# Sign and low bits of the weights as two 16-bit halves of one word, joined in one VectorE pass; plan priorities redone

## The chip, the core and the metric

The kernel runs on one core of a Trainium2 chip. A core has five engines that work side by side, each through its own instructions in order: TensorE (PE in the profile; its weight loads are PEld), VectorE (DVE), ScalarE (ACT), GpSimd (POOL) and SyncE (SP), which here only issues DMAs. The time is device microseconds of one execution. Medians of three runs are compared; the profile is one further execution, recorded instruction by instruction.

## The reference

The inputs and weights are 64-bit floats. Eight batches of 576 positions with 8 heads of 64 go through attention with a sliding window of 64, and the result, 4608 tokens of 512, goes through a layer with 1024 hidden units:

```python
scores = np.where(mask, scale * (q @ kT), -1e9)     # 0 <= i - j < 64
attn = exp(scores - max); attn /= sum + 1e-9
x = (attn @ v) ...                                  # 4608 x 512
h = x @ w_in                                        # 512 x 1024
e = exp(h - max(h)); sm = e / (sum(e) + 1e-9)
solu = h * sm
ln = (solu - mean) / sqrt(var + 1e-6) * g_ln
return ln @ w_out                                   # 1024 x 512
```

q, k and v reach the chip as 32-bit floats; w_in and w_out reach it as raw 64-bit words, and the kernel converts them itself.

## The kernel before

The tokens are cut into 36 tiles of 128. For tile t, `scores` puts q times k into PSUM (pS), `softmax` takes the minimum of the masked and negated scores per head (DVE, tile sS), the exponential (ACT, L480) and the division by the sum (POOL, L498; DVE for tile 0). `transposes` turns the eight blocks of sS, by TensorE (L533) for tiles 0 to 3 and by DMA from tile 4 on, into PT. `values` multiplies PT by v (L559), and ACT copies the result out as xH. `moe_in` multiplies xH by w_in into pH (L590 in plain 32-bit form for tiles 0 to 2, L603 in three rounded passes from tile 3 on). `moe_norm` takes the maximum (DVE, L618), the exponential (ACT, L620), the product with its sum (DVE, L623) and the normalisation. pH has one buffer, so L590 of the next tile waits until L623 has read it. `moe_transpose` turns the result, and `moe_out` multiplies it by w_out into pO (L724 for tiles 0 and 1, L737 after).

The weights come in eight blocks of 128 rows by 1024, blocks 0 to 3 for w_in and 4 to 7 for w_out; block 0 is handled in two halves of 512. A 64-bit word has two 32-bit words, `lo` and `hi`. A 32-bit float is made from them so, in `weight_block`:

- ACT writes |hi| times a power of two into the tile w (L351, `Abs`);
- POOL multiplies hi by zero in place, which leaves its sign (L360);
- DVE clips w from above (L362), shifts it left by 3 and ORs the sign in (L365), and shifts lo right by 29 and ORs that in (L368).

From tile 3 on the products run with weights split into a rounded part H and a rest L: `split` has ACT write H (L392 for w_in, L397 for w_out) and DVE the rest (L393, L399), 16 of each.

The order of each engine is found at build time. `Plan` gets each operation with a cost; it gives each a due time back from TensorE's order, adds a number from the table HINTS for some tiles, and plays the engines through, each of which takes the ready operation that is due first. The order found is written out as it is. SP issues DMAs in one queue: q and k of a tile (qk, 640 KB), v (512 KB), weight blocks (raw, 1 MB each, four buffers), the outputs. A raw block's load into a buffer waits for the last reader of the block that was there; the load of qk of tile t waits for the scores of tile t-3.

Of the kernel before, what the change touches and what calls it, by code (L numbers as in the profile page):

```python
# [19 lines left out]
P = 128  # L20
# [16 lines left out]
    ("DVE", "rec", 0, 0): 5100, ("DVE", "w", 0, 0): 2850, ("PE", "pS", 2, 0): 800, ("POOL", "e", 0, 0): 37550,
    ("POOL", "mst", 0, 0): -6350, ("ACT", "H", 0, 1): 850, ("DVE", "sS", 0, 1): 1100, ("DVE", "w", 0, 1): 200,
    ("PE", "pS", 0, 1): -59100, ("DVE", "w", 0, 2): 6350, ("PE", "pS", 0, 2): -14500,
    ("ACT", "yH", 0, 3): 57400, ("DVE", "PT", 0, 3): -29050, ("DVE", "y", 0, 3): 26250,  # L40
    ("DVE", "e", 0, 4): 2600, ("DVE", "rec", 0, 4): -4750, ("DVE", "sS", 0, 4): -3400,
# [185 lines left out]
def tile_window_attention_solu_moe(  # L227
# [672 lines left out]
```

## Time and profile before

| | us |
|---|---|
| median of three runs | 512.44 (512.27 to 513.65) |
| the profiled execution | 512.81 |
| its span, first to last instruction | 510.6 |
| mean granted TensorE clock over the span | 0.997 |

The span is the stretch that the profile shows; about 2.2 us of the execution's time lie around it. A row of a timeline gives start, duration, engine, line, what it writes and reads, how often, and in brackets how long the engine was idle before and what it waited for. TensorE's matmuls overlap, and their ends are modelled, so what a matmul costs is read from one start to the next. An L590 product of 128 by 512 stands in the trace as two records.

### The profile page before, as it was taken

The numbers are of one execution on the slowest core, as the hardware profiler recorded it, in microseconds if no ns is written. First come the engines' busy times: TensorE is split into PE (matmuls) and PEld (weight loads), VectorE is DVE, ScalarE is ACT, GpSimd is POOL, SyncE is SP. The second block draws the span as 40 slices with busy tenths as digits, with TensorE's granted clock in tenths as the row PEclk, the third lists the DMA queues.
The fourth block names the chain that finished last, engine by engine and source line by source line (L and its number), as shares of the span: only waits on it lengthen the run. The fifth ranks groups of instructions, "written<-read, shape, count | busy, mean of one in ns | idle before, by whom it ended". The sixth has DMA issues, their size and how long they took to land.

```text
span 510.6 us, 11601 instructions
## 1 busy us (share of the span) xinstructions
PE 492.0 (96%) x4064; PEld 392.5 (77%) x4064; DVE 406.0 (80%) x1176; ACT 355.7 (70%) x960; POOL 311.4 (61%) x566
## 2 busy tenths in 40 slices
PE   2889999999999999999999999999999999999996
PEld 1445576888888888888888888888888888888885
DVE  4988997979797979797878897877888879977531
ACT  5588795868686868676776867685959586855331
POOL 4389467574757574747474858484748485945430
PEclk9989999999999999999999999999999999999999
DMA  8994346978888878687989696969795969554201
GB/s 320 418 419 164 114 110 113 249 160 147 185 218 147 227 187 217 166 219 170 219 146 248 146 246 148 247 146 234 127 268 134 248 132 232 124 125 103 83 22 42
DMA packets 150762, 94.09 MB, mean 184 GB/s; under 512 B 135088, under 2 KB 135344, under 8 KB 150320
## 3 DMA queue, kind: packets, MB, share of 16 engines
q1 hardware_dynamic: 150704, 93.35, 72.5%
q8 instruction: 32, 0.52, 0.5%
q14 instruction: 26, 0.21, 0.1%
HBM read 50.86 MB, written 9.44 MB: 118 GB/s over the span
## 4 chain that ended last, share of the span: by engine, by line
PE 92%; DVE 3%; ACT 1%; issue 0%; ACTq 0%
PE pO L737 36%; PE pH L603 35%; PE pO L559 7%; PE pS L460 6%; PE pH L590 4%; PE pO L724 3%; PE pS L700 1%; DVE mst L618 0%; ACT e L620 0%; DVE w L368 0%; DVE e L623 0%; DVE sS L475 0%; DVE yL L711 0%; DVE w L365 0%; PE pS L533 0%
## 5 line engine op out<-in xcount | busy, mean ns | idle before, releaser
L498 POOL TENSOR_SCALAR sS<-sS,rec 128x128 f32<-128x128 f32 x280 | 147.2, 544 | 11.6 <-DVE rec L496 8.1
L480 ACT ACTIVATE sS<-sS,nmx 128x128 f32<-128x128 f32 x288 | 111.4, 389 | 2.0 <-DVE nmx L475 1.9
L737 PE MATMUL pO<-w_outH,yH 128*128 128x512 f32 x272 | 108.2, 398 | 0.0
L737 PE MATMUL pO<-w,yH 128*128 128x512 f32 x272 | 106.1, 390 | 0.0
L603 PE MATMUL pH<-w_inH,xH 128*128 128x512 f32 x264 | 103.7, 393 | 0.0
L603 PE MATMUL pH<-w,xH 128*128 128x512 f32 x264 | 101.8, 389 | 0.0
L737 PE MATMUL pO<-w_outH,yL 128*128 128x512 f32 x272 | 83.9, 390 | 0.0
L512 ACT COPY raw<-sS 128x1024 uint16<-128x1024 uint16 x64 | 66.8, 1046 | 23.0 <-POOL sS L498 23.0
L603 PE MATMUL pH<-w_inH,xL 128*128 128x512 f32 x264 | 81.9, 389 | 0.0
L640 POOL TENSOR_SCALAR e<-e,mst 128x512 f32<-128x512 f32 x72 | 68.9, 966 | 3.9
L632 POOL TENSOR_SCALAR mst<-mst 128x1 f32<-128x1 f32 x36 | 17.9, 497 | 79.2 <-ACT sq L629 42.9
L618 DVE TENSOR_REDUCE mst<-pH 128x1 f32<-128x1024 f32 x36 | 44.0, 1221 | 26.7 <-PE pH L603 24.6
L522 DVE COPY PT<-raw 128x1024 uint16<-128x1024 uint16 x64 | 49.8, 788 | 17.8 <-DMA raw<-raw 17.4
L573 ACT CAST xH<-pO 128x512 fp32r<-128x512 f32 x33 | 19.3, 585 | 64.0 <-PE pO L559 63.9
L737 PEld LDWEIGHTS pO<-w_outH,yH 128*128 128x128 f32 x272 | 51.0, 188 | 12.7 <-issue 2.4
L737 PEld LDWEIGHTS pO<-w_outH,yL 128*128 128x128 f32 x272 | 51.1, 188 | 10.9
L737 PEld LDWEIGHTS pO<-w,yH 128*128 128x128 f32 x272 | 51.1, 188 | 10.0
L603 PEld LDWEIGHTS pH<-w_inH,xH 128*128 128x128 f32 x264 | 49.6, 188 | 11.1 <-issue 0.3
L603 PEld LDWEIGHTS pH<-w_inH,xL 128*128 128x128 f32 x264 | 49.6, 188 | 10.6 <-issue 0.2
L603 PEld LDWEIGHTS pH<-w,xH 128*128 128x128 f32 x264 | 49.6, 188 | 10.4 <-issue 0.2
L626 POOL TENSOR_SCALAR mst<-mst 128x1 f32<-128x1 f32 x36 | 16.2, 451 | 65.6 <-DVE mst L623 59.7
L629 ACT ACTIVATE sq<-e,mst 128x1024 bf16<-128x1024 f32 x36 | 41.4, 1150 | 19.5 <-POOL mst L626 19.5
(71 smaller groups left out, 850.5 us busy)
## 6 DMA issues: line engine op xcount, KB each, us to landing
qk<-qk SPq DMA_DIRECT2D x36, 640.0 KB, 6.0
v<-vS SPq DMA_DIRECT2D x36, 512.0 KB, 4.6
y<-ot SPq DMA_DIRECT2D x35, 256.0 KB, 2.5
raw<-w_out SPq DMA_DIRECT2D x4, 1024.0 KB, 11.6
raw<-w_in SPq DMA_DIRECT2D x3, 1024.0 KB, 11.1
raw<-raw SPq DMA_TRANSPOSE x126, 2.8
raw<-w_in SPq DMA_DIRECT2D x2, 512.0 KB, 6.0
y<-ot SPq DMA_DIRECT2D x2, 128.0 KB, 1.7
```

Of the source, the lines that this page charges most:

```text
L460: nc.tensor.matmul(PS(t, p // 2)[half * WIN:(half + 1) * WIN, r, p], q[rs, p, half * WIN:(half + 1) * WIN], keys, start=True, stop=True)
L480: plan.op("ACT", 390, lambda h=h: nc.scalar.activation(SS(t)[:, h], SS(t)[:, h], AF.Exp, bias=cols("nmx", h), scale=-1.0, accum_out=cols(" ...
L498: plan.op(engine, cost, lambda h=h: v.tensor_scalar(SS(t)[:, h], SS(t)[:, h], rec()[:, h:h + 1], 0.0, ALU.mult, ALU.add), [R], [("sS", t, ...
L512: plan.op("ACT", 1050, lambda x=x: nc.scalar.copy(XP(t)[:, x], SS(t)[:, 4 * x:4 * x + 4].bitcast(U16).rearrange("p h (n w) -> p w (h n)", ...
L522: plan.op("DVE", 740, lambda x=x: nc.vector.tensor_copy(PT(t)[:, 4 * x:4 * x + 4].bitcast(U16).rearrange("p h (n w) -> p h w n", w=2), XP( ...
L559: nc.tensor.matmul(PX(t, p)[r * D:(r + 1) * D, p, ks], V(t, half)[:, h * D:(h + 1) * D], PT(t)[:, h, ks], start=True, stop=True)
L590: plan.op("PE", 860, lambda c=c, x=x: nc.tensor.matmul(PH(t)[:, x * 512:(x + 1) * 512], XH(t)[:, c], W32(c)[:, x], start=(c == 0), stop=(c ...
L603: plan.op("PE", 235, lambda n=n, c=c, d=d, x=x, w=w: nc.tensor.matmul(PH(t)[:, d * 512:(d + 1) * 512], x(t)[:, c], WH(c, d) if w is WH els ...
L618: plan.op("DVE", 1225, lambda: nc.vector.tensor_reduce(nmax(), PH(t), axis=AX.X, op=ALU.max, negate=True), [("pH", t)], [key(0)])
L629: plan.op("ACT", 1150, lambda: nc.scalar.activation(T("sq", t, [P, DFF], BF16), E(t), AF.Square, bias=nmean(), scale=1.0, accum_out=ss()), ...
L640: plan.op("POOL", 770, lambda h=h, hs=hs: nc.gpsimd.tensor_scalar(E(t)[:, hs], E(t)[:, hs], nmean(), kk(), ALU.add, ALU.mult), [key(4), ke ...
L737: plan.op("PE", 235, lambda n=n, f=f, i=i, x=x, y=y, w=w: nc.tensor.matmul(PO(), y(t)[:, f], w(i, x), start=(n == 0), stop=(n == len(passe ...
```

## The change

ACT now makes the low bits: a pass of type Copy scales the low word, read as an unsigned number, by 2^-29 and subtracts nearly a half, so that conversion to a 16-bit integer leaves the top three bits, and writes them into the lower half of the low word. POOL writes the sign, as 16-bit float zero with a sign, into the upper half of the same word. So the low word holds sign and low bits in place, and DVE needs one pass to shift w and OR that word in. POOL's pass now waits for ACT's low pass instead of the `Abs` pass. Block 0 has its two low passes, then its two `Abs` passes. HINTS is a new table; nothing else is changed.

```diff
 HINTS = {
-    ("ACT", "H", 0, 0): -5500, ("ACT", "w", 0, 0): -5050, ("DVE", "mst", 0, 0): 11450,
...
+    ("ACT", "raw", "w", 0): -53950, ("PE", "pH", 0, 36): -89650, ("DVE", "sS", 0, 0): -45650,
...
-MASKED = (0, 1, 2, 3, 4, 5, 6, 7)
+JOINED = (0, 1, 2, 3, 4, 5, 6, 7)
...
+        def piece(y, w, dtype):
+            return raw().bitcast(dtype).rearrange("p a n (k w) -> p a n k w", w=2)[:, y, :, 0, w]
...
-            masked = i in MASKED
-            if not masked:
+            joined = i in JOINED
+
+            def absolute(x=x, ab=ab, R=R, W=W):
+                plan.op("ACT", ab, lambda x=x: nc.scalar.activation(
+                    tf()[:, x], hi()[:, x].bitcast(F32), AF.Abs, scale=EXP_SCALE), [R], [W])
+
+            if not joined:
+                absolute()
+            else:
                 plan.op("ACT", ab + 12, lambda x=x: nc.scalar.activation(
-                    lo()[:, x], lo()[:, x].bitcast(U32), AF.Copy, bias=-0.47, scale=255 / 256 * 2.0 ** -29), [R], [B])
+                    piece(x, 0, U16), lo()[:, x].bitcast(U32), AF.Copy, bias=-0.47, scale=255 / 256 * 2.0 ** -29),
+                    [R], [B])
+                absolute()
...
-                plan.op("POOL", 660, lambda y=y: nc.gpsimd.tensor_scalar(
-                    hi()[:, y].bitcast(F32), hi()[:, y].bitcast(F32), 0.0, 1.0, ALU.mult, ALU.mult), [R, W], [S + (y,)])
+                plan.op("POOL", 660, lambda y=y, joined=joined: nc.gpsimd.tensor_scalar(
+                    piece(y, 1, BF16) if joined else hi()[:, y].bitcast(F32),
+                    hi()[:, y].bitcast(F32), 0.0, 1.0, ALU.mult, ALU.mult),
+                    [R, B] if joined else [R, W], [S + (y,)])
...
-            if masked:
+            if joined:
                 plan.op("DVE", n + 200, lambda x=x: nc.vector.scalar_tensor_tensor(
-                    t()[:, x], t()[:, x], 3, hi()[:, x], ALU.logical_shift_left, ALU.bitwise_or),
-                    [R, *D], [W], port=True)
+                    t()[:, x], t()[:, x], 3, lo()[:, x], ALU.logical_shift_left, ALU.bitwise_or),
+                    [R, B, *D], [W], port=True)
+            else:
                 plan.op("DVE", n + 200, lambda x=x: nc.vector.scalar_tensor_tensor(
-                    t()[:, x], lo()[:, x], 29, t()[:, x], ALU.logical_shift_right, ALU.bitwise_or),
+                    t()[:, x], t()[:, x], 3, hi()[:, x], ALU.logical_shift_left, ALU.bitwise_or),
                     [R], [W], port=True)
```

What the change and the new table do to the order is seen at three places. In the changed file L371 is ACT's low pass, L365 its `Abs`, L378 POOL's sign, L382 the clip and L385 the join; L607 is the old L590, L550 the old L533, L477 the old L460, L576 the old L559. The number after a tile's name is the block or tile; pS_73 and pS_74 take the transposes of tiles 1 and 2.

VectorE at the weights of w_in, before (L362 clip, L365 sign, L368 low bits):

```order
L362 TENSOR_SCALAR w_1_177<-w_1_177 128x1024
L365 SCALAR_TENSOR_TENSOR w_1_177<-w_1_177,raw_1_113 128x1024
L498 TENSOR_SCALAR sS_0_137<-sS_0_137,rec_0_169 128x128
L368 SCALAR_TENSOR_TENSOR w_1_177<-raw_1_113,w_1_177 128x1024
L362 TENSOR_SCALAR w_2_206<-w_2_206 128x1024
L365 SCALAR_TENSOR_TENSOR w_2_206<-w_2_206,raw_2_115 128x1024
```

The same place now:

```order
L382 TENSOR_SCALAR w_1_225<-w_1_225 128x1024
L385 SCALAR_TENSOR_TENSOR w_1_225<-w_1_225,raw_1_113 128x1024
L382 TENSOR_SCALAR w_2_249<-w_2_249 128x1024
L385 SCALAR_TENSOR_TENSOR w_2_249<-w_2_249,raw_2_115 128x1024
L382 TENSOR_SCALAR w_3_259<-w_3_259 128x1024
```

Block 2 is finished ahead of the minima of tile 1; before, its last pass stood behind those minima and behind block 3.

TensorE from the end of tile 0's hidden product (pH_0) to tile 1's (pH_1), before:

```order
L590 MATMUL pH_0_217<-w_2_206,xH_0_213 128x512 x2
L590 MATMUL pH_0_217<-w_3_243,xH_0_213 128x512 x2
L533 MATMUL pS_73_356<-ident_73,sS_1_253 128x128 x4
L460 MATMUL pS_3_361<-qk_3_245 64x128 x16
L559 MATMUL pO_37_385<-PT_1_381,v_1_149 64x64 x8
L533 MATMUL pS_73_356<-ident_73,sS_1_253 128x128 x4
L559 MATMUL pO_73_424<-PT_1_381,v_1_149 64x64 x8
L533 MATMUL pS_74_436<-ident_73,sS_2_315 128x128 x4
L590 MATMUL pH_1_447<-w_0_140,xH_1_413 128x512 x2
```

The same place now:

```order
L607 MATMUL pH_0_251<-w_3_259,xH_0_238 128x512 x2
L550 MATMUL pS_73_347<-ident_73,sS_1_269 128x128 x4
L477 MATMUL pS_3_359<-qk_3_261 64x128 x8
L550 MATMUL pS_73_347<-ident_73,sS_1_269 128x128 x4
L576 MATMUL pO_37_381<-PT_1_357,v_1_148 64x64 x8
L477 MATMUL pS_3_359<-qk_3_261 64x128 x8
L576 MATMUL pO_73_406<-PT_1_357,v_1_148 64x64 x8
L550 MATMUL pS_74_418<-ident_73,sS_2_310 128x128 x4
L607 MATMUL pH_1_429<-w_0_168,xH_1_404 128x512
L550 MATMUL pS_74_418<-ident_73,sS_2_310 128x128 x4
L607 MATMUL pH_1_429<-w_0_168,xH_1_404 128x512
```

The scores of tile 3 are in two halves; the first still stands ahead of most of tile 1's work. The second half of pS_74, which stood behind pH_1, now stands inside it.

ScalarE from the exponential of tile 1's hidden layer (e_1) on, before:

```order
L620 ACTIVATE e_1_533,mst_1_498<-pH_1_447,mst_1_498 128x1024
L569 COPY xH_2_521<-pO_74_536 128x256
L538 COPY PT_3_567<-pS_75_547 128x512
L480 ACTIVATE sS_4_552,sm_4_570<-sS_4_552,nmx_4_553 128x128 x3
L392 CAST w_inH_98<-w_2_206 128x512
L480 ACTIVATE sS_4_552,sm_4_570<-sS_4_552,nmx_4_553 128x128 x5
L392 CAST w_inH_98<-w_2_206 128x512
L392 CAST w_inH_98<-w_1_177 128x512 x2
```

The same place now (L637 is the old L620, L586 the old L569, L497 the old L480, L646 the square, L414 the old L397, L409 the old L392):

```order
L637 ACTIVATE e_1_529,mst_1_497<-pH_1_429,mst_1_497 128x1024
L586 COPY xH_2_548<-pO_38_516 128x256
L586 COPY xH_2_548<-pO_74_531 128x256
L365 ACTIVATE w_6_559<-raw_6_341 128x1024
L365 ACTIVATE w_7_566<-raw_7_379 128x1024
L371 ACTIVATE raw_7_379<-raw_7_379 128x1024
L371 ACTIVATE raw_5_256<-raw_5_256 128x1024
L497 ACTIVATE sS_4_540,sm_4_583<-sS_4_540,nmx_4_541 128x128 x8
L646 ACTIVATE sq_1_601,mst_1_497<-e_1_529,mst_1_497 128x1024
L414 ACTIVATE w_outH_99<-w_5_495,g_sb_100 128x512 x2
L409 CAST w_inH_98<-w_0_168 128x512 x2
```

Four passes of the weight blocks now stand behind this exponential, where none stood, and all eight casts of w_in follow them; before, block 0's two casts were ahead of it.

## Rows read from the trace of the kernel before

**Rows 1.** The page: busy us (share of the span) and instructions of each engine.

```profile
PE 492.0 (96%) x4064; PEld 392.5 (77%) x4064; DVE 406.0 (80%) x1176; ACT 355.7 (70%) x960; POOL 311.4 (61%) x566
```

**Rows 2.** TensorE's waits: who waited for whom, us in total, times, longest.

```profile
PE pH L590 <- DVE w L368: 1.7, 1, 1.7
...
PE pS L460 <- PE pS L460: 0.4, 1, 0.4
```

**Rows 3.** Timeline of TensorE, 14 to 50 us: start, duration, instruction, idle before.

```profile
26.77 5.37 PE L590 MATMUL pH<-w,xH 128*128 128x512 f32 x8 [1.73 <-DVE w L368]
31.97 0.60 PE L533 MATMUL pS<-ident,sS 128*128 128x128 f32 x4
32.50 1.10 PE L460 MATMUL pS<-qk 64*64 64x128 f32 x32
33.53 0.69 PE L559 MATMUL pO<-PT,v 128*64 128x64 f32 x16
34.15 0.66 PE L533 MATMUL pS<-ident,sS 128*128 128x128 f32 x4
...
36.59 7.03 PE L590 MATMUL pH<-w,xH 128*128 128x512 f32 x16
43.46 0.60 PE L533 MATMUL pS<-ident,sS 128*128 128x128 f32 x4
...
47.70 2.84 PE L590 MATMUL pH<-w,xH 128*128 128x512 f32 x6 [0.35 <-DVE mst L623]
```

**Rows 4.** Busy time by stretch; then granted clock (PEclk), DMA share, GB/s.

```profile
24.00:27.00 3.00, 1.27 (x3) 0.47 (x4) 2.97 (x10) 2.06 (x7) 0.87 (x1) 1.00 1.03 416
27.00:30.00 3.00, 3.00 (x4) 1.04 (x4) 2.88 (x18) 2.92 (x15) 2.63 (x7) 0.51 1.02 422
```

**Rows 5.** Groups by line and form, whole span: busy us, mean ns, idle before.

```profile
L512 ACT COPY raw<-sS 128x1024 uint16<-128x1024 uint16 x64 | 66.8, 1046 | 23.0 <-POOL sS L498 23.0
...
L360 POOL TENSOR_SCALAR raw<-raw 128x512 f32<-128x512 f32 x16 | 11.9, 767 | 15.0 <-ACT w L351 15.0
L368 DVE SCALAR_TENSOR_TENSOR w<-raw,w 128x1024 int32<-128x1024 int32 x7 | 9.0, 1284 | 0.1
L365 DVE SCALAR_TENSOR_TENSOR w<-w,raw 128x1024 int32<-128x1024 int32 x7 | 8.6, 1226 | 0.5
L351 ACT ACTIVATE w<-raw 128x1024 f32<-128x1024 f32 x7 | 8.0, 1149 | 5.8 <-DMA raw<-w_in 5.4 <-DMA raw<-w_out 0.4
...
L368 DVE SCALAR_TENSOR_TENSOR w<-raw,w 128x512 int32<-128x512 int32 x2 | 1.7, 848 | 0.1
...
L351 ACT ACTIVATE w<-raw 128x512 f32<-128x512 f32 x2 | 1.3, 651 | 4.8 <-DMA raw<-w_in 4.8
```

**Rows 6.** Busy time by stretch of 10 us: PE, PEld, DVE, ACT, POOL; clock, DMA, GB/s.

```profile
20.00:30.00 10.00, 8.27 (x62) 3.88 (x62) 9.75 (x41) 8.80 (x35) 4.80 (x9) 0.85 1.03 418
30.00:40.00 10.00, 9.32 (x89) 5.61 (x88) 8.77 (x28) 8.44 (x26) 9.26 (x16) 0.98 1.02 417
...
60.00:70.00 10.00, 10.00 (x36) 6.45 (x35) 9.74 (x34) 10.00 (x27) 6.61 (x14) 1.00 0.52 138
```

**Rows 7.** ScalarE's timeline, 10.8 to 32.5 us.

```profile
10.60 0.38 ACT L480 ACTIVATE sS<-sS,nmx 128x128 f32<-128x128 f32 x1
...
12.87 0.56 ACT L538 COPY PT<-pS 128x512 f32<-128x512 f32 x1
...
19.50 1.17 ACT L351 ACTIVATE w<-raw 128x1024 f32<-128x1024 f32 x1 [3.88 <-DMA raw<-w_in]
...
24.05 0.35 ACT L569 COPY xH<-pO 128x256 f32<-128x256 f32 x1
24.84 1.14 ACT L351 ACTIVATE w<-raw 128x1024 f32<-128x1024 f32 x1 [0.45 <-DMA raw<-w_out]
```

**Rows 8.** The one qk load issued at 19.3 us (L419): its row, its landing.

```profile
L419 SPq DMA_DIRECT2D qk<-qk x1: 418/418/418, 19.3 to 19.3; - x1
...
DMA to landing us min/median/max: 10.9/10.9/10.9
```

More of the change, by code (lines that the diff above doesn't have):

```diff
@@ L35 @@
 HINTS = {
-    ("ACT", "H", 0, 0): -5500, ("ACT", "w", 0, 0): -5050, ("DVE", "mst", 0, 0): 11450,
[L37 to L41, printed above, removed]
@@ L51 @@
-    ("POOL", "sS", 0, "e"): 900,
+    ("ACT", "raw", "w", 0): -53950, ("PE", "pH", 0, 36): -89650, ("DVE", "sS", 0, 0): -45650,
+    ("ACT", "sS", 0, 0): -5250, ("DVE", "rec", 0, 0): -44950, ("ACT", "raw", "w", 1): -32750,
+    ("ACT", "raw", "w", 2): -68150, ("ACT", "PT", 0, 0): -64150, ("DVE", "sS", 0, 1): 46450,
+    ("ACT", "w", 0, 3): -82400, ("ACT", "w", 0, 4): 20250, ("ACT", "raw", "w", 5): 36650,
+    ("ACT", "w", 0, 5): 31000, ("ACT", "raw", "w", 7): 7800, ("DVE", "w", 0, 7): -2600,
+    ("PE", "pS", 0, 2): -15500, ("DVE", "sS", 0, 2): -88000, ("ACT", "mst", 0, 0): 5900,
@@ new lines @@
+    ("POOL", "e", 0, 0): 160100, ("POOL", "sS", 0, 3): 46750, ("PE", "pH", 0, 1): 30400,
+    ("ACT", "mst", 0, 1): 48650, ("POOL", "e", 0, 1): 65650, ("ACT", "PT", 0, 2): 32150,
+    ("ACT", "sS", 0, 4): 45700, ("DVE", "rec", 0, 4): -14900, ("ACT", "raw", "P", 4): -30000,
+    ("PE", "pO", 1, 2): 33200, ("PE", "pS", 2, 3): -57850, ("DVE", "mst", 0, 2): 74900,
+    ("ACT", "e", 0, 2): -111850, ("DVE", "yH", 0, 0): -10800, ("DVE", "sS", 0, 5): 45200,
+    ("DVE", "rec", 0, 5): -148600, ("POOL", "sS", 0, 5): 54600, ("ACT", "raw", "P", 5): -20900,
@@ L52 @@
+    ("ACT", "H", 0, 0): -13700, ("ACT", "H", 0, 1): -13300, ("ACT", "H", 0, 2): -1600,
+    ("DVE", "mst", 0, 3): -10150, ("ACT", "raw", "P", 6): 107950, ("DVE", "PT", 0, 5): 14200,
+    ("POOL", "e", 0, 4): -34850, ("DVE", "sS", 0, 7): -172950, ("DVE", "rec", 0, 7): -10550,
[9 rows of a table added]
 }
@@ L350, in weight_block @@
             ab = 1139 if i else 644
-            plan.op("ACT", ab, lambda x=x: nc.scalar.activation(
-                tf()[:, x], hi()[:, x].bitcast(F32), AF.Abs, scale=EXP_SCALE), [R], [W])
-            masked = i in MASKED
-            if not masked:
+            joined = i in JOINED
[5 more added lines that the diff above has]
+            else:
                 plan.op("ACT", ab + 12, lambda x=x: nc.scalar.activation(
-                    lo()[:, x], lo()[:, x].bitcast(U32), AF.Copy, bias=-0.47, scale=255 / 256 * 2.0 ** -29), [R], [B])
+                    piece(x, 0, U16), lo()[:, x].bitcast(U32), AF.Copy, bias=-0.47, scale=255 / 256 * 2.0 ** -29),
+                    [R], [B])
+                absolute()
             halves = [x] if i == 0 else [0, 1]
-            D = [S + (y,) for y in halves] if masked else []
-            for y in halves if masked else []:
-                plan.op("POOL", 660, lambda y=y: nc.gpsimd.tensor_scalar(
-                    hi()[:, y].bitcast(F32), hi()[:, y].bitcast(F32), 0.0, 1.0, ALU.mult, ALU.mult), [R, W], [S + (y,)])
+            D = [S + (y,) for y in halves]
+            for y in halves:
+                plan.op("POOL", 660, lambda y=y, joined=joined: nc.gpsimd.tensor_scalar(
+                    piece(y, 1, BF16) if joined else hi()[:, y].bitcast(F32),
+                    hi()[:, y].bitcast(F32), 0.0, 1.0, ALU.mult, ALU.mult),
+                    [R, B] if joined else [R, W], [S + (y,)])
             plan.op("DVE", n // 3 * 2 + (18 if i else 78), lambda x=x: nc.vector.tensor_scalar_min(
                 tf()[:, x], tf()[:, x], EXP_HI * EXP_SCALE), [W], [W], port=True)
-            if masked:
+            if joined:
+                plan.op("DVE", n + 200, lambda x=x: nc.vector.scalar_tensor_tensor(
+                    t()[:, x], t()[:, x], 3, lo()[:, x], ALU.logical_shift_left, ALU.bitwise_or),
+                    [R, B, *D], [W], port=True)
+            else:
                 plan.op("DVE", n + 200, lambda x=x: nc.vector.scalar_tensor_tensor(
```

13 lines of the change are left out of this document (removed), and 12 rows, old and new, of the table HINTS.

## The prediction, made before the changed kernel was run

> **What bounds the kernel now.** I read the page's busy times first: TensorE is busy for 96% of the span, the next engine, VectorE, for 80% [rows 1]. So the end moves only if TensorE has less to do, which it does not, or waits less. Its waits come next, and after the first 15 us they are few: 1.7 us of L590 for L368, 0.4 us of L460 for a PSUM buffer [rows 2], 0.35 us of L590 for L623. The timeline puts the first at 26.77 us, the last at 47.70 us [rows 3]; from there on TensorE goes on to the end with waits of well under 1 us. What the change can give is therefore how much earlier than 47.70 us the hidden product of tile 2 starts; later it can only lose.
>
> The wait at 26.77 us has a second price. The granted clock is 1.00 (2.4 GHz) over 24 to 27 us and 0.51 (1.2 GHz) over the next 3 us, after TensorE had stood for 1.73 us [rows 4]. The eight L590 records from 26.77 us last until 31.97 us, 5.20 us; at tile 1 sixteen of them take 43.46 - 36.59 = 6.87 us, so eight take 3.44 us [rows 3]. The fall cost 1.76 us.
>
> Last I looked at what brings the data. DMA's share is full and it moves 418 and 417 GB/s from 20 to 40 us [rows 6], so what is issued later lands later. The qk load of tile 3, issued at 19.3 us, lands 10.9 us later, at 30.2 us [rows 8]; before it lie the weight blocks 0 to 5.
>
> **The change part by part.** *VectorE loses a pass* (L368) per block: 7 x 1.284 + 2 x 0.848 = 10.7 us [rows 5]; the pass that stays differs from L365, 1.226 us, only in the word it reads. *ScalarE gains a pass* per block. It reads and scales as L351 does, so I take 7 x 1.149 + 2 x 0.651 = 9.35 us [rows 5]. Nothing in the trace writes 16-bit pieces eight bytes apart; ScalarE's pass over as many elements with a packed 16-bit result, L512, takes 1.046 us [rows 5], which is the lower end, and twice L351, 2.30 us, the upper. *GpSimd* keeps sixteen passes, 0.767 us each [rows 5], now with a 16-bit result: between half and one and a half of that, I take the same. They wait for ScalarE's low pass now, and the joins wait for them; of block 4, the first stands ahead of the division of tile 2 in GpSimd's order, which TensorE's transposes need. By the times below its low pass is done at 29.1 us, while GpSimd still divides tile 1. Up to 30 us all this lies behind a landing and costs nothing; without that cover it is at most 2 x 0.4 us a block.
>
> *Where the moved work ends up.* ScalarE after tile 0's exponentials (the last of them begin at 10.60 us, so free at 11.0): two Abs halves to 12.2, low pass of block 1 to 13.2, two PT copies of 0.56 us [rows 7] to 14.2, low 2 to 15.4, Abs 1 to 16.5, xH copy (0.35) to 16.8, Abs 2 to 17.9, xH to 18.2, Abs 3 when its block has landed, 19.50 us [rows 7], to 20.7, low 3 to 21.8, eight exponentials at 0.385 us to 24.9, eight more to 28.0, low 4 to 29.1, the PT copy of tile 1 to 29.6. VectorE, idle more than before, then joins block 1 by 18.4 us, block 2 by 20.3 us, and block 3 by 24.4 us, behind the minima of tile 1. TensorE has the first half of xH at 16.8 us and 17.4 us behind the scores of tile 1; its eight products of pH_0 and the scores of tile 2 come one after the other and end at about 26.7 us, against 31.97 us before [rows 3]. So the wait for L368 is gone, 5 us are won at this point, and one must ask what is late next.
>
> It is the landing. TensorE's order puts the scores of tile 3 right behind the first transposes of tile 1, and their qk lands at 30.2 us. The transposes follow GpSimd's division and are through by about 28.3 us. The loads ahead of this qk in SP's order are the same; blocks 4 and 5, whose issue waits for the joins of blocks 0 and 1, go out at about 15 and 18.5 us (13.2 and 18.85 before), with DMA full all the while, so I leave the landing where it is. A new wait of about 2 us arises there, and with the short stop ahead of the transposes TensorE does half a microsecond of work between 26.7 and 30.2 us.
>
> From the landing to the end of tile 1's hidden product, at the full clock [rows 3]: scores 33.53 - 32.50 = 1.03; second transposes 32.50 - 31.97 = 0.53; two halves of values at 34.15 - 33.53 = 0.62; both halves of the transposes of tile 2, 2 x 0.53; the product, 6.87. The sum is 10.73 us, and the product ends at 30.2 + 10.73 = 40.95 us. Before, it ended at 43.46 us: 2.5 us earlier. What these need is ready: the PT copy at 29.6 us for 31.8, GpSimd's divisions of tile 2 (begun at about 30.1 us, 0.36 us a head) for 33.5 us and later.
>
> From there to the start of tile 2's product both kernels need the same chain, maximum, exponential, L623, as pH has one buffer: 47.70 - 43.46 = 4.24 us [rows 3]. That one half of tile 2's transposes is already done does not shorten it.
>
> Then the clock. TensorE stands longer at 26.7 to 30.2 us than the 1.73 us that lost the clock before. I take one fall of the same size in the stretch that follows, in which TensorE's own work sets the pace: 1.76 us. What is left is 2.5 - 1.76 = 0.75 us. On the profiled execution, 510.6 us of span with 2.2 us around it, that is 512.81 - 0.75 = 512.06 us; the median of the runs is 0.37 us lower, so 511.7 us.
>
> After 47 us ScalarE has to carry more. Between the exponential of tile 1's hidden layer and the first rounded xH (tile 3) the new order gives it 18.8 us without a pause, by the durations of its lines before; that ends, with xL 0.7 us behind, about 0.45 us ahead of TensorE's first need. Before, it was busy for the whole of 60 to 70 us [rows 6]. I cost this at nothing, with that cover.
>
> **Rules weighed.** The trace shows the fall in one place of one execution only [rows 4]. The Trainium skill (TensorE: Matmul & The Clock Gate, The HAM clock gate) says that the watch over TensorE's activity runs freely and does not begin anew with a kernel, so the moment of a fall shifts from run to run. By it the same wait may cost nothing in one execution and more in the next, which no row here can show; both are rivals below, priced from rows.
>
> Of the added passes the rows say 1.149 us on ScalarE against 1.284 us on VectorE [rows 5]. The Trainium skill (ScalarE: Activation LUTs, Rules for kernel authors) speaks against such a move: simple arithmetic belongs on VectorE, up to about three times faster there. By that rule the change would pay 9.35 us of ScalarE for 3.6 us of VectorE, and the last rival would be the likeliest; the rows do not bear it out for this pass.
>
> **The rivals.** *The clock holds.* If the idle time is cut by the moment at which the clock is judged, or the transposes suffice as activity, the 1.76 us are not lost: 512.44 - 2.5 = 509.9 us. For it: the wait is broken by transposes. Against: a shorter stop sufficed before.
>
> *The clock stays low twice as long.* If the stop straddles that moment, two stretches are lost: 3.5 us, and 512.44 - 2.5 + 3.5 = 513.4 us. For it: over 3 us with almost no work. Against: in the trace the next stretch, full of work, brought it back.
>
> *ScalarE becomes the bound* (the slower side). Place: from the exponential of tile 1's hidden layer to the first rounded xH. Price: what its passes take beyond 0.45 us in all goes straight to TensorE; the same holds at the PT copy of tile 1 from 1.7 us over four low passes, thus from 1.6 us a pass. At 2.3 us a pass TensorE would be 2.9 us late there and 1.9 us later: 512.44 - 2.5 + 1.76 + 4.8 = 516.5 us; half way it is 514.2 us, which I give it. Against: such passes are paced by elements in every row of ScalarE. For: 10.00 busy of 10 at 60 to 70 us [rows 6].
>
> *VectorE's saving is not there*, as reading a word written in halves slows the join: three joins could each take 1.1 us longer before pH_0 ended at 30.2 us, so the time stays that of the forecast, 511.7 us, and it has no chance of its own.
>
> **How the numbers follow.** Forecast 0.50 (511.7, with 510.9 to 512.6 for itself), clock holds 0.25 (509.9), clock low twice as long 0.10 (513.4), ScalarE 0.15 (514.2). The range 509.7 to 513.9 leaves out under half of the case in which the clock holds and over half of the ScalarE case. Faster by over 0.3%, which is 1.5 us and about what a measurement of this kernel can tell from no change: all of the case in which the clock holds and a sixth of the forecast, 0.33. Slower by over 0.3%: over half of the ScalarE case, a fifth of the low clock, a tenth of the forecast, 0.16. Within: 0.51.
>
> **What would show it.** Right: pH_0 ends at 26 to 28 us; TensorE's wait for L368 is replaced by one for the qk load, ending near 30.2 us; the granted clock falls once between 28 and 35 us; the product of tile 2 starts at 46.5 to 47.2 us; low passes near 1.15 us. Wrong: a wait for ScalarE before the first L603 or for PT of tile 1; a landing of that qk well before 29 us; new waits after 100 us.

## The result and the profile after

The changed kernel takes 519.88 us (median; 518.86 to 520.24) against 512.48 us for the kernel before in the same series: a ratio of 1.0135, 95% interval 1.0118 to 1.0152. The prediction, 511.7 us with a range up to 513.9 us, missed it, on the slower side. The profiled execution took 519.9 us, 518.1 us of it span (before: 510.6 us).

The page's busy times of the changed kernel, against [rows 1]:

```profile
PE 494.7 (95%) x4064; PEld 394.5 (76%) x4064; DVE 396.3 (76%) x1167; ACT 372.7 (72%) x969; POOL 318.0 (61%) x566
```

VectorE lost 9.7 us where 10.7 were worked out. ScalarE gained 17.0 us where 9.35 were priced, and GpSimd 6.6 us where nothing was. The groups by line and form (busy us, mean ns of one, idle before) show which instructions, to be held against [rows 5]:

```profile
L378 POOL TENSOR_SCALAR raw<-raw 128x512 bf16<-128x512 f32 x16 | 22.2, 1471 | 16.4 <-ACT raw L371 16.4
L371 ACT ACTIVATE raw<-raw 128x1024 uint16<-128x1024 uint32 x7 | 17.3, 2515 | 0.0
L385 DVE SCALAR_TENSOR_TENSOR w<-w,raw 128x1024 int32<-128x1024 int32 x7 | 10.0, 1429 | 4.6 <-POOL raw L378 4.3
...
L365 ACT ACTIVATE w<-raw 128x1024 f32<-128x1024 f32 x7 | 8.0, 1167 | 0.0
...
L371 ACT ACTIVATE raw<-raw 128x512 uint16<-128x512 uint32 x2 | 2.7, 1328 | 4.7 <-DMA raw<-w_in 4.7
```

The low pass (L371) takes 2.515 us, over twice the Abs pass (L365) that reads as many elements from the same block. GpSimd's sign (L378) takes 1.471 us where it took 0.767. TensorE's waits after the first 15 us, against [rows 2]:

```profile
PE pS L550 <- ACT PT L555: 1.8, 1, 1.8
PE pO L576 <- ACT PT L555: 1.7, 1, 1.7
PE pH L607 <- DVE w L385: 1.5, 2, 1.2
PE pO L741 <- DVE yH L722: 1.3, 1, 1.3
```

Their places are in TensorE's timeline, 26 to 56 us (start, duration, instruction, idle before), against [rows 3]:

```profile
28.97 1.99 PE L607 MATMUL pH<-w,xH 128*128 128x512 f32 x4 [1.22 <-DVE w L385]
31.52 1.38 PE L550 MATMUL pS<-ident,sS 128*128 128x128 f32 x4 [0.57 <-POOL sS L515]
32.84 0.67 PE L477 MATMUL pS<-qk 64*64 64x128 f32 x16
35.29 1.09 PE L550 MATMUL pS<-ident,sS 128*128 128x128 f32 x4 [1.79 <-ACT PT L555]
...
48.37 0.67 PE L477 MATMUL pS<-qk 64*64 64x128 f32 x16
...
52.82 3.67 PE L607 MATMUL pH<-w,xH 128*128 128x512 f32 x8 [0.84 <-DVE mst L640]
```

pH_0 ends near 30.9 us, 4 us later than predicted. The scores of tile 3 at 32.84 us wait for nothing, as their qk landed at 30.6 us. Then TensorE stands for the PT copy of tile 1. ScalarE's timeline, in stretches, shows why:

```profile
13.00 2.49 ACT L371 ACTIVATE raw<-raw 128x1024 uint16<-128x1024 uint32 x1
...
22.22 2.51 ACT L371 ACTIVATE raw<-raw 128x1024 uint16<-128x1024 uint32 x1
...
29.16 0.40 ACT L497 ACTIVATE sS<-sS,nmx 128x128 f32<-128x128 f32 x1 [0.44 <-DVE nmx L492]
...
32.26 2.47 ACT L371 ACTIVATE raw<-raw 128x1024 uint16<-128x1024 uint32 x1
34.48 0.67 ACT L555 COPY PT<-pS 128x512 f32<-128x512 f32 x1
```

Four low passes lie ahead of that copy (the one not shown began at 16.29 us), each 1.35 us longer than priced: 5.4 us. The copy ends at 35.15 us; the prediction had it at 29.6. That the two differences agree is partly chance: at the end of the third pass, 24.73 us, ScalarE is 2.9 us behind the predicted 21.8 us, since part of the delay went into the 1.3 us for which the prediction had it idle ahead of block 3; then its exponentials stand 0.80 us (up to 25.53) and 0.44 us for VectorE's minima, the second time behind a join that had waited 0.71 us for a sign. The windows of that stretch (busy us of PE, PEld, DVE, ACT, POOL; granted clock; DMA share; GB/s) show the second price, against [rows 4]:

```profile
31.00:34.70 3.70, 1.91 (x20) 0.98 (x20) 1.59 (x3) 3.70 (x10) 2.80 (x8) 1.00 1.02 420
34.70:41.60 6.90, 6.31 (x58) 4.79 (x59) 4.14 (x22) 5.56 (x17) 5.50 (x11) 0.51 0.67 255
```

ScalarE is busy for all of 31.0 to 34.7 us, TensorE for half of it, and TensorE then runs 6.9 us at 0.51 (1.2 GHz). The last loss is at 64.2 us. First GpSimd's timeline, then VectorE's:

```profile
56.52 5.71 POOL L378 TENSOR_SCALAR raw<-raw 128x512 bf16<-128x512 f32 x4 [3.22 <-ACT raw L371]
```

```profile
59.04 1.96 DVE L385 SCALAR_TENSOR_TENSOR w<-w,raw 128x1024 int32<-128x1024 int32 x1 [2.33 <-POOL raw L378]
62.27 1.23 DVE L385 SCALAR_TENSOR_TENSOR w<-w,raw 128x1024 int32<-128x1024 int32 x1 [1.26 <-POOL raw L378]
...
63.48 0.68 DVE L722 TENSOR_TENSOR yH<-pS,g_sb 128x512 f32<-128x512 f32 x1
```

GpSimd waits for a low pass, makes four signs in 5.71 us, two joins wait for them on VectorE, and yH, queued behind the joins, reaches TensorE 1.30 us late.

So the 7.5 us of span are, up to rounding: the product of tile 2 starts at 52.82 instead of 47.70 us, 5.1; from there to the last matmul 460.4 instead of 458.8 us, 1.6, of which 1.3 is the wait for yH; and 0.7 us more behind the last matmul, of which more below.

### The profile page after: what moved, and what is told of

It is laid out like the page before. It is cut to its first block, busy times and chain, and to the rows that moved or that the text cites. A ratio compares the mean times of both kernels' runs of the same rounds, so it can differ in the third digit from the quotient of the medians.

```text
span 518.1 us, 11615 instructions
## 1 busy us (share of the span) xinstructions
PE 494.7 (95%) x4064; PEld 394.5 (76%) x4064; DVE 396.3 (76%) x1167; ACT 372.7 (72%) x969; POOL 318.0 (61%) x566
## 4 chain that ended last, share of the span: by engine, by line
PE 85%; ACT 8%; POOL 3%; DVE 2%; DMA 1%; issue 1%; SPq 0%; ACTq 0%; POOLq 0%
PE pO L754 35%; PE pH L620 35%; PE pO L576 7%; PE pS L477 6%; ACT raw L371 3%; POOL raw L378 2%; ACT sS L497 1%; PE pO L741 1%; DMA raw<-w_in 1%; ACT w L365 1%; PE pS L717 1%; DVE w L385 0%; ACT e L637 0%; ACT PT L555 0%; ACT w_inH L409 0%
## 5 line engine op out<-in xcount | busy, mean ns | idle before, releaser
L497 ACT ACTIVATE sS<-sS,nmx 128x128 f32<-128x128 f32 x288 | 111.4, 390 | 1.2 <-DVE nmx L492 1.2
L620 PE MATMUL pH<-w_inH,xH 128*128 128x512 f32 x264 | 103.5, 392 | 0.0
L620 PE MATMUL pH<-w,xH 128*128 128x512 f32 x264 | 101.9, 390 | 0.0
L620 PE MATMUL pH<-w_inH,xL 128*128 128x512 f32 x264 | 82.1, 390 | 0.2 <-DVE xL L591 0.2
L657 POOL TENSOR_SCALAR e<-e,mst 128x512 f32<-128x512 f32 x72 | 67.4, 945 | 3.7
L635 DVE TENSOR_REDUCE mst<-pH 128x1 f32<-128x1024 f32 x36 | 44.0, 1222 | 30.6 <-PE pH L620 25.3
L590 ACT CAST xH<-pO 128x512 fp32r<-128x512 f32 x33 | 19.3, 585 | 63.3 <-PE pO L576 63.3
L754 PEld LDWEIGHTS pO<-w_outH,yL 128*128 128x128 f32 x272 | 51.1, 188 | 10.8
L620 PEld LDWEIGHTS pH<-w_inH,xH 128*128 128x128 f32 x264 | 49.6, 188 | 11.0 <-ACT xH L590 0.4
L620 PEld LDWEIGHTS pH<-w_inH,xL 128*128 128x128 f32 x264 | 49.6, 188 | 10.9 <-DVE xL L591 0.7
L620 PEld LDWEIGHTS pH<-w,xH 128*128 128x128 f32 x264 | 49.6, 188 | 10.4 <-issue 0.2
L646 ACT ACTIVATE sq<-e,mst 128x1024 bf16<-128x1024 f32 x36 | 41.4, 1151 | 19.6 <-POOL mst L643 19.6
```

What stands on the lines that cost most here:

```text
L497: plan.op("ACT", 390, lambda h=h: nc.scalar.activation(SS(t)[:, h], SS(t)[:, h], AF.Exp, bias=cols("nmx", h), scale=-1.0, accum_out=cols(" ...
L590: plan.op("ACT", 560, lambda: nc.scalar.copy(XH(t), PX(t)), [("pO", NTILE + t)], [("xH", t)])
L620: plan.op("PE", 235, lambda n=n, c=c, d=d, x=x, w=w: nc.tensor.matmul(PH(t)[:, d * 512:(d + 1) * 512], x(t)[:, c], WH(c, d) if w is WH els ...
L635: plan.op("DVE", 1225, lambda: nc.vector.tensor_reduce(nmax(), PH(t), axis=AX.X, op=ALU.max, negate=True), [("pH", t)], [key(0)])
L646: plan.op("ACT", 1150, lambda: nc.scalar.activation(T("sq", t, [P, DFF], BF16), E(t), AF.Square, bias=nmean(), scale=1.0, accum_out=ss()), ...
L657: plan.op("POOL", 770, lambda h=h, hs=hs: nc.gpsimd.tensor_scalar(E(t)[:, hs], E(t)[:, hs], nmean(), kk(), ALU.add, ALU.mult), [key(4), ke ...
```

## The experiments

Theory after the result: a 16-bit write whose elements lie eight bytes apart is itself slow, on ScalarE and on GpSimd, and everything else follows from the two lengths. Rivals: the conversion from uint32, or the write in place, is slow; or the new priorities lose the time by themselves.

**The passes by themselves** (`passes_alone`: the kernel before, with passes behind its last output).

```
+ act(packed(U16), U, **C)      # L884; 2 bytes apart
+ act(spaced(U16), U, **C)      # L885; 4 bytes apart, other buffer
+ act(full(I32), U, **C)        # L886
+ act(half(0, 0, U16), U, **C)  # L888; 8 bytes apart, in place: the change
+ act(lo, U, **C)               # L890; whole word, in place
+ sign(packed / half(0, 1) BF16, F32 in place)  # L892, L895, L897
```

> The kernel before, with single passes behind its end, one after the other, nothing else running: ScalarE over 128x1024 and GpSimd over two times 128x512, with the same reads and different writes. Theory 1 (pieces): what costs is writing 16-bit elements that are not packed, a part of a 32-bit word at a time. Then the unsigned low word written as packed 16 bit, as 32-bit integer (in place or elsewhere) or as 32-bit float takes 1.05 to 1.2 us, written as 16 bit eight or four bytes apart about 2.5 us, in place or not, and so does the absolute value with a 16-bit result eight bytes apart; GpSimd takes 0.64 us for 32-bit or packed results and about 1.3 us for spaced 16-bit ones. Theory 2 (conversion): what costs is reading an unsigned 32-bit integer; then every ScalarE pass that reads it takes about 2.5 us, whatever it writes, and the absolute value with a spaced 16-bit result 1.15 us; GpSimd's excess has no reason in it. Theory 3 (in place): only passes that write a piece of the word they read are slow, 2.5 us; pieces elsewhere 1.15 us.

The timeline of that stretch; each row is two passes:

```profile
515.21 2.25 ACT L884 ACTIVATE y<-raw 128x1024 uint16<-128x1024 uint32 x2
517.48 2.72 ACT L885 ACTIVATE y<-raw 128x1024 uint16<-128x1024 uint32 x2
...
527.39 4.99 ACT L888 ACTIVATE raw<-raw 128x1024 uint16<-128x1024 uint32 x2
527.45 1.26 POOL L892 TENSOR_SCALAR y<-raw 128x512 bf16<-128x512 f32 x2 [31.12 <-ACT raw L887]
...
537.41 2.23 ACT L890 ACTIVATE raw<-raw 128x1024 int32<-128x1024 uint32 x2
...
541.98 2.47 POOL L895 TENSOR_SCALAR raw<-raw 128x512 bf16<-128x512 f32 x2 [10.54 <-ACT raw L891]
```

The first theory held. Neither the conversion (L884, L890) nor the place (L890) costs anything: 1.1 us. The same 1024 elements as 16-bit pieces cost 1.1 us packed, 1.36 us at 4 bytes and 2.5 us at 8 bytes; GpSimd's 512 cost 0.63, and 1.24 us at 8 bytes. An Abs of F32 values into such pieces took 2.47 us as well, so the source plays no part.

**Which property of the write it is** (`steps_alone`: passes of 512 elements, all from the same packed F32 values, into elements of 2 or 4 bytes at several steps, on three engines).

> The kernel before with 34 further passes of 512 elements after its last output, which nothing uses: ScalarE, VectorE and GpSimd each read the same close-packed F32 values and write bf16 2, 4, 8 and 16 bytes apart and F32 4, 8 and 16 bytes apart, two of each; then ScalarE reads such values. Theory 1, a 16-bit write pays by its step, whatever is read: on ScalarE 0.55 us a pass of 512 at 2 bytes, 0.67 at 4, 1.24 at 8 (half of the 1.11, 1.34 and 2.48 us of 1024), more at 16; F32 the same at every step; GpSimd 0.65, 0.77, 1.32. Theory 2, the price lay in the read and the write lying together in one 8-byte pair: with the source elsewhere 8 bytes cost no more than 4. For VectorE neither says anything.

The timeline; two passes a row. L871 to L874 write bf16 at 2, 4, 8 and 16 bytes, L876 and L877 F32 at 8 and 16; L878 and L880 are VectorE's bf16 at 2 and 8, L887 GpSimd's at 8:

```profile
513.90 1.29 ACT L871 ACTIVATE raw<-y 128x512 bf16<-128x512 f32 x2
515.22 1.57 ACT L872 ACTIVATE raw<-y 128x512 bf16<-128x512 f32 x2
516.83 2.70 ACT L873 ACTIVATE raw<-y 128x512 bf16<-128x512 f32 x2
519.56 4.96 ACT L874 ACTIVATE raw<-y 128x512 bf16<-128x512 f32 x2
...
525.87 1.35 ACT L876 ACTIVATE raw<-y 128x512 f32<-128x512 f32 x2
527.25 2.23 ACT L877 ACTIVATE raw<-y 128x512 f32<-128x512 f32 x2
529.52 0.89 DVE L878 TENSOR_SCALAR raw<-y 128x512 bf16<-128x512 f32 x2 [22.34 <-ACT raw L877]
...
531.42 1.50 DVE L880 TENSOR_SCALAR raw<-y 128x512 bf16<-128x512 f32 x2
...
541.99 2.73 POOL L887 TENSOR_SCALAR raw<-y 128x512 bf16<-128x512 f32 x2
```

The step of the write sets the price, whatever is read. Counted in elements, a step of two costs a fifth more with 16 bits and next to nothing with F32; a step of four makes the pass 2.1 times as long for bf16 (2.70 of 1.29 us) and 1.7 times for F32 (2.23), and one of eight nearly doubles it again (4.96). So the first theory held for 16 bits, but not where it had F32 the same at every step. VectorE pays too, 1.50 against 0.89 us, and GpSimd 2.73 against 1.33. Reading at 8 bytes cost next to nothing: two passes over bf16 or F32 at that step took 1.35 us, two over packed bf16 1.29. Both kernels of passes alone were executed once.

**Each half of the change as a whole word, and both.** The word's width in what is written is the only edit:

```
  low_as_whole_word:    - piece(x, 0, U16)   + lo()[:, x]            (ScalarE)
  sign_as_whole_word:   - piece(y, 1, BF16)  + lo()[:, y].bitcast(F32)  (GpSimd)
  both_as_whole_words:  both of them
```

> The changed kernel with ScalarE's low pass writing a whole 32-bit integer over the low word; GpSimd still writes the sign as a 16-bit piece into its upper half, and the order is the same. Theory 1: the low pass is back at about 1.15 us, ScalarE is 9 x 1.3 us freer, the PT copy of tile 1 is at its place near 30 us, and the time is 511 to 513 us, where the prediction saw it; GpSimd's 1.3 us passes stay and cost up to 1 us. Theory 2: the pass still takes 2.5 us and the time stays at 520 us.

> The changed kernel with GpSimd's sign pass alone written as a whole F32 word (over the low word, so the low bits are left out); ScalarE's low pass stays a 16-bit half of about 2.5 us. Theory 1, the two long passes cost about half of the loss each (the low pass written whole gave 516.15 of 519.88): near 516 us, with the wait for the PT copy of tile 1 (1.8 us) still there. Theory 2, both lie in one chain and ScalarE's is the one that ends last, so GpSimd's length is hidden behind it: 518.5 us or more. Theory 3, GpSimd's pass is the heavier one, and ScalarE's hurts only through it: 514 us or less.

> The changed kernel with both short passes written as whole 32-bit words: ScalarE's low pass as int32 into the low word, GpSimd's sign pass as F32 over the same word (so the low bits are left out of the weights). Same passes, same order of dependences, same priorities; only the width of what is written differs. Alone at the end of a program those passes took 1.10 and 0.64 us against 2.48 and 1.32 us as spaced 16-bit halves. Theory 1, the length of the two passes is the whole loss: low pass about 1.15 us, sign 0.65 to 0.85 us, no PT wait over 0.5 us, and the time that the prediction worked out with such lengths, 511.7 us (510 to 513.5). Theory 2, the new priorities carry a loss of their own (waits stay where they are although the passes are short): 514.5 us or more.

Medians and ratios to the kernel before: low whole 516.15 us (1.0061, 1.0043 to 1.0080), sign whole 517.77 us (1.0104, 1.0087 to 1.0121), both 511.21 us (0.9977, 0.9964 to 0.9990). Alone they give back 0.74 and 0.31% of 1.35, together 1.58%: not additive, since with either one long TensorE still stood in the same stretch. Low whole kept a wait of 1.55 us for a join at 27.52 us, sign whole the waits for PT; both still lost the clock. Neither came at a time that one of its theories gave. Against both whole, the long signs alone cost 4.9 us and the long low passes alone 6.6. With both whole the first theory held: the changed order and priorities are as they were, and they carry no loss once the passes are short. The groups of `both_as_whole_words`, then TensorE's timeline, 15 to 50 us:

```profile
L378 POOL TENSOR_SCALAR raw<-raw 128x512 f32<-128x512 f32 x16 | 12.9, 825 | 14.9 <-ACT raw L371 14.9
...
L371 ACT ACTIVATE raw<-raw 128x1024 int32<-128x1024 uint32 x7 | 8.0, 1159 | 0.0
```

```profile
23.62 4.56 PE L607 MATMUL pH<-w,xH 128*128 128x512 f32 x10
...
30.35 0.67 PE L477 MATMUL pS<-qk 64*64 64x128 f32 x16 [1.73 <-DMA qk<-qk]
30.95 0.66 PE L550 MATMUL pS<-ident,sS 128*128 128x128 f32 x4
...
41.25 0.67 PE L477 MATMUL pS<-qk 64*64 64x128 f32 x16
...
45.70 4.53 PE L607 MATMUL pH<-w,xH 128*128 128x512 f32 x10 [0.93 <-DVE mst L640]
```

This is the course that the prediction described for passes of 1.149 and 0.767 us: pH_0 done at 28 us, then a wait for the qk of tile 3, which landed at 30.2 us. The window of that stop (columns as above) has TensorE busy for 2.27 of 4 us, and the clock held:

```profile
27.00:31.00 4.00, 2.27 (x24) 1.20 (x22) 1.79 (x4) 3.68 (x10) 4.00 (x12) 1.00 1.02 420
```

**The priorities alone, and the path alone.** `new_path_old_table` puts the table of before into the changed kernel, `old_path_new_table` the table of after into the kernel before.

```
  HINTS = { ... }   # the entries of before, or the new ones
```

> The changed kernel with the table of priorities from before. If the slow passes make the loss, it stays, 517 to 523 us, and may grow, as the old table knows nothing of ScalarE's extra pass. If the new table makes the loss, it falls to 512 to 514 us.

> The kernel before with the new table of priorities, the three passes on VectorE as they were. If the slow passes make the loss, 511 to 515 us. If the new table makes it, 517 us and more.

525.31 us (1.0243, 1.0224 to 1.0262) and 532.42 us (1.0387, 1.0372 to 1.0403). Both lie above what the expectations gave for slow passes (523 and 515 us), so neither run tells the table from the passes: each table loses with the other path, and that the new one costs nothing rests on `both_as_whole_words`. Under the old one TensorE waits 4.2 us for a PT copy of tile 0, under the new one 4.9 us for a division on GpSimd. From TensorE's timelines, the first kernel, then the second:

```profile
15.78 1.12 PE L568 MATMUL pO<-PT,v 128*64 128x64 f32 x16 [4.21 <-ACT PT L547]
```

```profile
34.69 1.53 PE L541 MATMUL pS<-ident,sS 128*128 128x128 f32 x4 [4.89 <-POOL sS L506]
```

**The planner told of the true lengths** (`true_costs`).

```
- plan.op("ACT", ab + 12, ...                 - plan.op("POOL", 660, ...
+ plan.op("ACT", 2500 if i else 1320, ...     + plan.op("POOL", 1325, ...
```

> The changed kernel with the two planned costs put right: ScalarE's low pass 2500 ns instead of 1151 (1320 for the half block, instead of 656), GpSimd's sign 1325 instead of 660; priorities and instructions unchanged. Theory 1, a good part of the loss is the plan, which puts the PT copy of tile 1 behind a pass that it holds to be half as long: the PT wait of 1.8 us goes, near 517 us. Theory 2, the priorities were fitted to the other costs and the order falls apart: 522 us or more. Theory 3, the order of the engines hardly depends on these costs: 519 to 521 us.

533.58 us (1.0407, 1.0372 to 1.0442): its second theory held. The priorities shift due times that are worked out from these costs, so new costs under old priorities make another order, in which one wait for a PT copy alone takes 8.4 us. The experiment says nothing on how good an order fitted to the true costs would be.

**The qk load earlier** (`both_whole_qk_earlier`, on `both_as_whole_words`).

```
-    prep(5); load(3)
+    load(3, range(1)); prep(5); load(3, range(1, 2))
```

> As both_as_whole_words (low bits left out of the weights), with the qk load of tile 3 issued ahead of that of weight block 5 instead of behind it. In both_as_whole_words TensorE waits 1.73 us for that load, which lands at 30.2 us. Theory 1, what the shorter join gives beyond 511.2 us is lost in this wait: the load lands near 28 us, the wait goes and the time falls to 509 to 510 us. Theory 2, the next thing is as late (weight block 5 lands later, or the product of tile 2 waits for its normalised rows anyway): 511 us or more.

519.41 us (1.0133, 1.0110 to 1.0156). The wait for qk is gone, yet the product of tile 2 starts at 45.27 instead of 45.70 us: the landing was the last limit by only 0.4 us, and the PT copies are next. The 519.41 us say little of that: elsewhere the new plan has a weight remainder late, and TensorE stands 5.7 us for it up to 98.6 us.

**The halves four bytes apart, everything computed.** First in a buffer of their own, with the planner told of it (`word_close_packed`) and not (`word_close_packed_same_order`), then in the block's weight tile (`word_in_its_place`).

```
  word_close_packed, word_close_packed_same_order:
+ "hw": 2  (RINGS);   piece() and the join's word: T("hw", i, [P, 2, 512])
  word_in_its_place:
  piece(): raw(), step 8 bytes    ->  W32(i), step 4 bytes
  Abs and clip: write W32(i)      ->  write the raw block's low words
  join: t = (t << 3) | lo         ->  t = (lo << 3) | t
```

> The changed kernel with the two halves written into a word buffer of their own, two buffers in turn, in which the words lie 4 bytes apart instead of 8; everything is computed. Alone at the end of a program such 16-bit halves, 4 bytes apart, took 1.34 us on ScalarE and 0.77 us on GpSimd (2.48 and 1.32 us at 8 bytes). Theory 1, the price is set by the step of a 16-bit write and by nothing else of the change: low pass about 1.35 to 1.4 us, sign 0.77 to 0.95 us, and a time of 512 to 514 us, near the 511.7 us that shorter passes gave in the prediction's working plus 0.2 us for each of the passes that are waited for. Theory 2, two word buffers are too few: the low pass of a block waits for the join two blocks earlier, and the time stays at 516 us or more.

> As word_close_packed (halves in a word buffer of their own, words 4 bytes apart, two buffers in turn, everything computed), but the planner is not told of the two buffers, so that every engine has its instructions in exactly the order of the changed kernel. Theory 1, the 515.29 us of word_close_packed against 511.21 us with whole words came from the order that the planner made of the ring of two: now low pass near 1.38 us, sign 0.8 to 0.95 us, 511.5 to 513 us, at best a little below the kernel before. Theory 2, the ring itself costs (a low pass waits on the chip for the join two blocks earlier), or the buffers moved to other addresses do: 514.5 us or more with the same order.

> Everything computed, every engine's instructions in the order of the changed kernel, no further buffer: the two 16-bit halves go into the block's own weight tile, where the words lie 4 bytes apart; the magnitudes are made and clipped in the low words of the raw block, and the join writes the weight tile. In word_close_packed_same_order GpSimd's sign passes waited 5.8 us in all for the join two blocks earlier, and the low passes began late. Theory 1, that ring of two buffers is what held it at 514.47 us: without it low passes of 1.36 and signs of 0.9 us (against 1.16 and 0.83 us as whole words, 511.21 us) leave 511.5 to 513 us, though VectorE's clip now steps over 8 bytes and takes perhaps 0.9 instead of 0.75 us. Theory 2, the slack at the PT copy of tile 1 is so thin that 0.2 us more a low pass and 0.1 us more a sign cost the 3 us by themselves: 514 us or more again.

515.29 us (1.0057, 1.0037 to 1.0077), 514.47 us (1.0034, 1.0022 to 1.0046), and 512.85 us (1.0005, 0.9993 to 1.0017). The first two fell between their theories; the order of the changed kernel gave back at most a little of the first one's loss, as the intervals overlap. With a ring of two buffers GpSimd's signs wait for joins (waits on GpSimd, 5 to 60 us, of the second kernel):

```profile
POOL hw L381 <- DVE w L388: 5.8, 2, 3.0
```

In the third kernel, without that ring, they wait for landings alone, and its first theory held. As it also moves the Abs pass and the clip to other words, that the ring held the second one back is read from the waits, not tried alone. Its groups, and its place in TensorE's timeline:

```profile
L378 POOL TENSOR_SCALAR w<-raw 128x512 bf16<-128x512 f32 x16 | 14.2, 915 | 10.6 <-DMA raw<-w_in 10.6
L371 ACT ACTIVATE w<-raw 128x1024 uint16<-128x1024 uint32 x7 | 9.4, 1367 | 0.1
```

```profile
32.44 0.63 PE L550 MATMUL pS<-ident,sS 128*128 128x128 f32 x4 [0.92 <-ACT PT L555]
...
47.17 3.24 PE L607 MATMUL pH<-w,xH 128*128 128x512 f32 x7 [0.93 <-DVE mst L640]
```

With 1.37 instead of 2.5 us a low pass and 0.92 instead of 1.47 us a sign the whole loss is gone, and the kernel is level with the one before. No version that computes everything beat the kernel before; the one that was 0.23% below it leaves the low bits out.

## Why the prediction was wrong, point by point

**The step that failed** is the term of ScalarE's added pass: "It reads and scales as L351 does, so I take 7 x 1.149 + 2 x 0.651 = 9.35 us", with twice L351, 2.30 us, as the upper end. It measured 17.3 + 2.7 = 20.0 us, 2.515 us a pass, above the upper end. GpSimd's term, 0.767 us with half as much more as its bound, failed in the same way: 1.471 us, and what it costs TensorE was put at nothing, where the long signs alone cost 4.9 us (516.15 against 511.21 us). Both were priced by what they read; what they write, 16-bit pieces four elements apart, sets their length. The prediction had noted that no row showed such a write, and then took the row of a pass that writes whole words; its "against" (passes are paced by elements in every row of ScalarE) rested on rows that all write packed results. The trace of the kernel before held a hint on another engine. VectorE's copies of 1024 16-bit elements are shorter where the result is packed (L666) than where it goes into every second half word (L679):

```profile
L666 DVE COPY raw<-e 128x1024 uint16<-128x1024 uint16 x62 | 43.5, 710 | 8.5 <-POOL e L640 8.4
L679 DVE COPY y<-raw 128x1024 uint16<-128x1024 uint16 x62 | 48.3, 802 | 5.8 <-DMA raw<-raw 5.4 <-DVE nmx L475 0.3
```

**The rival that came** is "ScalarE becomes the bound", at the second place that it named, the PT copy of tile 1. Margin 1.6 us a pass, four passes of 2.5 us: 3.6 us late. Measured: the second transposes start at 35.29 us instead of 30.2 + 1.03 = 31.23, 4.1 us late. From there to the product of tile 2 the changed kernel took 17.53 us. The prediction's terms for that are 9.70 + 4.24, plus 1.76 for the clock: 1.8 us too few. Together 5.9 us, which is 52.82 less the predicted 46.93 us. Of the 1.8 us, 0.6 are a step out of order: the prediction put both halves of the scores ahead of the second transposes, while TensorE's order has only the first there. So the margin was smaller than it said. With short passes these transposes start at 30.95 us, and against that they are 4.3 us late. Another 1.0 us is the clock, 0.2 the chain.

TensorE had stood for a PT copy of tile 1 in the kernel before, too, which the prediction's list of waits left out:

```profile
35.48 0.69 PE L559 MATMUL pO<-PT,v 128*64 128x64 f32 x16 [0.68 <-ACT PT L538]
```

The rival's chance of 0.15 and its 514.2 us were too low because the price was capped at 2.3 us and then halved; its own 516.5 us for 2.3 us already lay outside the range. With 2.515 us its working gives 512.44 - 2.5 + 1.76 + 3.8 + 2.3 = 517.8 us, and the kernel in which only the low passes are long took 517.77 us. That is in part luck, as the 2.3 us were put at the rival's other place. The 2.1 us that are left up to 519.88 us are those of the signs.

**Its other place** was wrong. At the first rounded xH TensorE waited only 0.2 us (for xL). The later loss is the 1.3 us for yH at 64.2 us, and it comes through GpSimd: it is 0.8 us with the low pass whole and gone with the sign whole. The prediction had written that a slower sign costs at most 2 x 0.4 us a block without cover, and had looked for that cover only up to 30 us.

**VectorE loses a pass:** right, 9.7 us of busy time against 10.7; the join at 62.27 us takes 1.23 us. That reading halves does not slow the join was right too; the mean of 1.429 us comes from joins that ran beside GpSimd's signs, like the 1.96 us at 59.04 us.

**The landing** of the qk of tile 3, 30.2 us: right, 30.6 in the changed kernel and 30.2 us in `both_as_whole_words`. In the changed kernel it was issued 4 us later, at 23.3 instead of 19.3 us, as the late join of block 1 held up block 5 ahead of it, and landed within 7.3 instead of 10.9 us. In the changed kernel it limits nothing, since TensorE comes later.

**From the landing to the end of tile 1's product,** 10.73 us at the full clock: 41.25 - 30.35 = 10.90 us in `both_as_whole_words`. The chain after it, 4.24 us: 4.45 us there and in the changed kernel.

**The clock.** One fall of 1.76 us was priced. In the changed kernel the same instructions take 48.37 - 35.29 = 13.08 us against 41.25 - 30.95 = 10.30 us in `both_as_whole_words`: 2.8 us lost, between the prediction's one and two stretches. In the profiled execution of that kernel the clock held at 1.00 from 19 us to the last matmul, in spite of a stop of 1.73 us, so for short passes the case "the clock holds" came. Its 509.9 us did not: 511.21 us. The product of tile 2 started 2.0 us earlier instead of 2.5. And those gains are counted from the profiled execution of the kernel before, in which the clock fell, but were taken off the median of executions, in most of which it cannot have fallen so: that fall is what takes its mean clock over the span to 0.997, while 45 of the 52 other executions of that kernel whose clock is on record have 0.999 or 1.000. So the same kernel keeps the clock there in most executions. What a fall there costs it in the end was not tried; the profiled execution took 512.81 us and the 45 a median of 512.43, which does not point to the whole 1.76 us.

**The end of the program** was not in the sum at all. From the start of the last matmul to the end of the span it takes 4.12 us before, 4.80 after, 4.59 in `both_as_whole_words` and 4.68 us in `word_in_its_place`. All of the difference lies behind the issue of the last output, 0.87 us after that matmul in each of them. Half of the 0.7 us does not reach the time: 1.8 us of it lie around the span in the changed kernel, 2.2 before. What lengthens the end was not tried and stays open.

**The rule on the placement of simple arithmetic** (the Trainium skill, ScalarE: Activation LUTs, Rules for kernel authors) would have called the direction. By the page, its figure of up to about three times is for bf16 and passes with one input. The passes over the weights read 32-bit words, so the 3.6 us of the prediction have no ground. For 16-bit copies of 1024 with one input this case has 1.05 us on ScalarE (L512, [rows 5]) and 0.71 on VectorE (L666). For passes with one input from F32 to bf16 `steps_alone` agrees in kind, two passes each: VectorE took 0.89 us where ScalarE took 1.29 (L878, L871), and 1.50 where it took 2.70 (L880, L873). The pass that VectorE lost has two inputs; it took 1.28 us, ScalarE's written packed 1.1 us. So the runs do not speak against the move itself, only against its write.

What is shown: that the two long passes cause the loss (undone together, 8.7 us go), that the write's step makes them long, and that the new order by itself loses nothing. Only read from the traces, not tried alone, is the share of the clock, and that of the signs' overlap with VectorE (below).

## What to carry to other kernels

Price an elementwise pass by what it writes as well as by what it reads: a 16-bit result scattered into every second word took twice as long as a whole word, or longer, on ScalarE and GpSimd, while the same halves laid into adjacent words cost a fifth more. Where no row shows an operation, twice the nearest row is no upper bound; a pass or two of the new form behind the kernel's end settles it. A table of priorities fits one set of durations: with the other path, with other costs or with one load moved it lost 5 to 20 us here.

## What the runs showed of the hardware that I had not expected

The price of a stepped write goes by the step in elements more than in bytes, and all three engines pay it: at four elements 1.35 us for 512 bf16 on ScalarE (packed 0.65), 1.37 on GpSimd (0.67), 0.75 on VectorE (0.45); at eight elements 2.48, 2.50 and 1.32 us. Stepped reads at 8 bytes cost next to nothing (0.68 us).

Signs on GpSimd and joins on VectorE that run at the same time slow each other. In `low_as_whole_word` the three joins of 1024 that ran wholly beside signs took 1.91 to 2.09 us and the other four 1.21 to 1.23; in `sign_as_whole_word`, where the signs are short and hardly overlap, all seven took 1.22 to 1.24 us. In the former a sign by itself took 1.33 us, four in a row beside VectorE's passes 6.91 us.

A stop of 1.73 us ending at 26.77 us was followed by the lower clock in the profiled execution of the kernel before [rows 3, 4], while in most others of that kernel it cannot have fallen so; one of the same length ending at 30.35 us in `both_as_whole_words` was not.
